# Decayed attention and a highway feed-forward on one core: a common ring of five PSUM banks, a written-out task order, and loads in pieces

## The chip, the cores and the metric

The kernel runs on one core of a Trainium2 chip. The metric is the time of one execution on the device, in microseconds (us), of the slowest core, which is the only one here. TensorE is called PE, VectorE DVE, ScalarE ACT, GpSimd POOL, and SP issues the transfers.

The executions scatter. The kernel before took 116.45 to 116.64 us in the three runs given at the start, but 114.9 to 119.2 us in the 33 runs made beside the experiments. So times are compared between kernels that ran on the same chip in the same session; where that wasn't possible, the text says so.

## The reference, cut to what matters

Four sequences of 768 positions with eight heads of 64 go through attention with a decay per head, in blocks of 64 with a running state. The output, as 3072 tokens of 512 features, goes through a highway layer.

```python
for b in range(nb):                                   # blocks of 64 positions
    intra = einsum('bhic,bhjc->bhij', qb, kb) * Dmask # scores, decayed, causal
    intra = einsum('bhij,bhjd->bhid', intra, vb)
    inter = einsum('bhid,bhde->bhie', qb * lam_pow, kv_state)
    out[:, :, sl] = intra + inter
    kv_state = lam_block * kv_state + einsum('bhsd,bhse->bhde', kb * rev_pow, vb)
...
H = maximum(x @ w_h, 0);  T = sigmoid(x @ w_t + b_t)  # x: 3072 x 512
return T * H + (1 - T) * x
```

## The kernel before

The tokens are taken in 12 chunks of 256, three to a sequence. Each chunk `n` passes through these tasks, on the engines named:

- load of k, q, v (SP), their cast or scaling to bf16 (`kb`, `qb`, `vs`: mostly POOL), transposition of k and q (PE) and copies `kT`, `qT` out of PSUM (ACT);
- scores (PE), masked by DVE into `m`; the products `inter` and `intra` into the tile `o` (PE), the state `kv` (PE) and its copy `ss` (ACT);
- copy of `o` to `xT` (ACT and DVE), then four feed-forward blocks `h`, `t` (PE), the sigmoid of `t` (ACT), `hmx` = max(h,0) − x (DVE), the product `th` = sigmoid × hmx (DVE for the first half, POOL for the second), the output turn x + th (PE), its copy `o_sb` (ACT), and the store (SP).

PSUM is divided into eight tiles of 512 fp32 values per partition, called banks below: scores own two, a ring of three (`"w"`) serves transpositions, blocks and turns, `o` has two and `kv` one.

```python
WB = 3
...
buf(("s", n, u), "s", [128, 2, 2, J, C], F32, pool=ps)          # scores: two banks of their own
buf((x + "tr", n, p), "w", [128, z // 2, J, C], bufs=WB, pool=ps)
buf((x, g, js[0]), "w", [128, 2, z * C], F32, bufs=WB, pool=ps) # h and t of a block
buf(("x", n, m, i), "w", [C, DM // parts_o], F32, bufs=WB, pool=ps)
```

The second is that a sigmoid whose product runs on DVE is written back into its PSUM bank, so this bank of the ring comes free only after block, sigmoid and product:

```python
def gate(g, js):
    return ("t_sb" if TH[js[0] // 2] == "POOL" else "t"), g, js[0]   # "t" is the PSUM tile
```

A list scheduler, run while the program is built, starts on each engine the task with the best key; the keys are in `K`.

```python
k = (max(0.0, s - free[e] - GAP), (t.key if t.key > -9 else 99)
     + SAME * (t.mode != last_mode) + WAIT * (s - free[e]))          # for PE
...
for t in plan(tasks):
    t.emit()
```

The loads: one transfer of 512 KB for each of k, q, v of a chunk (of 256 KB in the first two chunks), and 24 fills of four 128-column matmuls that warm PE up.

## Time and profile before

| | kernel before |
|---|---|
| time, median of 3 | 116.52 us |
| span of the profiled execution | 113.2 us |
| PE busy | 101.2 us (89%) |
| DVE, ACT, POOL busy | 67.7, 76.5, 69.6 us |
| instructions | 4880 |
| moved by DMA | 27.57 MB, mean 243 GB/s |

One of the page's costliest groups shows how a group is read: line, engine, operation, output<-inputs, shapes, count; then busy time and mean ns of one; then the engine's idle time before the group and what ended most of it.

```profile
L375 DVE TENSOR_TENSOR m<-s,tri 128x512 bf16<-128x512 f32 x48 | 31.6, 686 | 14.7 <-PE s L371 14.7
```

DVE stood idle 14.7 us in front of its masks, until the scores came from PE. This is room, not a limit. The limit is PE, and the prediction shows the views that say so.

Lines are told as L422 and the like. The ones that return are the block (L422 before, L293 after), the output turn (L444, L315), the transposition (L355, L223), scores (L371, L239), the mask (L375, L243), the product `th` (L438, L309), the state (L404, L272), the inter product (L384, L252), copies and casts on DVE and POOL (L306, L175), copies on ACT (L304, L173), loads (L341, L208) and stores (L456, L324).

### The profile page before, as it was taken

To read this page: it belongs to the slowest core of one execution; us is meant where nothing else is said; L and a number is where in the kernel's file an instruction comes from. 1 tells how busy PE (TensorE), PEld (TensorE's weight loads), DVE (VectorE), ACT (ScalarE), POOL (GpSimd) and SP (SyncE) were. 2 spreads that over 40 slices of the span, in tenths; PEclk is the share of its full clock that TensorE was granted. 3 is DMA by queue.
4 is the path that set the end of the run, shared out by engine and by line. 5 is a ranking of instruction groups with operands and counts; after the bars stand their busy time and mean duration, and the time that the engine had idled before them with its cause. 6 is when DMAs were issued, how large, how long until landed. Compare 5 with 4: busy or idle time off the path is not lost.

```text
span 113.2 us, 4880 instructions
## 1 busy us (share of the span) xinstructions
PE 101.2 (89%) x2145; PEld 88.9 (78%) x2145; DVE 67.7 (60%) x113; ACT 76.5 (68%) x146; POOL 69.6 (61%) x61
## 2 busy tenths in 40 slices
PE   4896576998897999999999999999999999998860
PEld 4895364778686788989889898998998989888750
DVE  0237756475266759658495676774966749764420
ACT  3595681556877676694879686967878667377550
POOL 6032337238999987979997997969597300404220
PEclk9999996799999999999999999999999999999999
DMA  0999999999999999999999999999951040403154
GB/s 9 255 298 291 311 329 349 302 263 300 279 296 291 336 352 306 293 288 298 307 320 310 285 340 294 333 285 298 337 184 53 11 180 6 184 7 148 37 208 162
DMA packets 43484, 27.57 MB, mean 243 GB/s; under 512 B 1348, under 2 KB 40520, under 8 KB 43464
## 3 DMA queue, kind: packets, MB, share of 16 engines
q1 hardware_dynamic: 43312, 27.27, 84.4%
q8 instruction: 16, 0.26, 1.0%
q14 instruction: 4, 0.03, 0.1%
q10 hardware_dynamic: 152, 0.01, 0.1%
HBM read 20.98 MB, written 6.29 MB: 241 GB/s over the span
## 4 chain that ended last, share of the span: by engine, by line
PE 72%; SPq 8%; DVE 7%; DMA 5%; ACT 3%; issue 2%; POOLq 1%; ACTq 0%
PE w L422 37%; PE w L444 9%; PE w L355 8%; SPq L341 7%; PE o L396 6%; DMA vf<-in_v_dram 5%; PE s L371 5%; PE o L384 5%; PE kv L404 4%; DVE m L375 3%; ACT w L435 2%; DVE xT L306 2%; DVE th L438 1%; SPq L300 1%; POOLq L602 1%
## 5 line engine op out<-in xcount | busy, mean ns | idle before, releaser
L422 PE MATMUL w<-xT,w_b 128*128 128x256 bf16 (+1 forms) x416 | 47.8, 267 | 1.4 <-DVE th L438 0.9
L422 PEld LDWEIGHTS <-w_b 128*128 128x128 bf16 x416 | 37.1, 99 | 6.5 <-issue 1.9
L375 DVE TENSOR_TENSOR m<-s,tri 128x512 bf16<-128x512 f32 x48 | 31.6, 686 | 14.7 <-PE s L371 14.7
L438 POOL TENSOR_TENSOR th<-t_sb,hmx 128x512 bf16<-128x512 bf16 (+1 forms) x13 | 14.0, 1080 | 21.2 <-DVE hmx L426 14.8
L349 POOL TENSOR_TENSOR qb<-qf,pow_q 128x1024 bf16<-128x1024 f32 (+1 forms) x13 | 22.1, 1703 | 7.8 <-DMA qf<-in_q_dram 7.7
L426 DVE SCALAR_TENSOR_TENSOR hmx<-w,xT 128x512 bf16<-128x512 f32 (+1 forms) x26 | 16.8, 647 | 10.0 <-PE w L422 5.2
L349 POOL TENSOR_TENSOR vs<-vf,pow_k 128x1024 bf16<-128x1024 f32 (+1 forms) x11 | 20.1, 1824 | 2.3 <-DMA vf<-in_v_dram 2.3
L450 ACT ACTIVATE o_sb<-w 128x512 f32<-128x512 f32 (+1 forms) x24 | 13.6, 587 | 5.3 <-PE w L444 5.0
L435 ACT ACTIVATE w<-w,bt_col 128x256 f32<-128x256 f32 (+1 forms) x26 | 11.2, 432 | 8.3 <-ACT kT L304 4.0
L304 ACT ACTIVATE qT<-w 128x1024 bf16<-128x1024 bf16 (+1 forms) x14 | 12.7, 904 | 4.8 <-PE w L355 4.8
L306 POOL CAST kb<-kf 128x1024 bf16<-128x1024 f32 (+1 forms) x11 | 11.0, 997 | 6.3 <-DMA kf<-in_k_dram 6.3
L304 ACT ACTIVATE kT<-w 128x1024 bf16<-128x1024 bf16 (+1 forms) x14 | 12.6, 896 | 1.9 <-PE w L355 1.9
L444 PE MATMUL w<-id,th 128*128 128x128 bf16 x96 | 12.9, 219 | 0.6 <-POOL th L438 0.6
L444 PE MATMUL w<-id,xT 128*128 128x128 bf16 x96 | 13.0, 220 | 0.4 <-DVE th L438 0.4
L438 DVE TENSOR_TENSOR th<-w,hmx 128x512 bf16<-128x512 f32 (+1 forms) x13 | 8.4, 645 | 6.3 <-ACT w L435 6.3
L435 ACT ACTIVATE t_sb<-w,bt_col 128x256 bf16<-128x256 f32 (+1 forms) x26 | 10.5, 461 | 2.4 <-PE w L422 2.4
L371 PE MATMUL s<-qT,kT 64*64 64x128 bf16 x384 | 11.4, 219 | 0.3 <-DVE m L375 0.3
L404 PE MATMUL kv<-vs,kb 64*64 64x64 bf16 x320 | 9.5, 197 | 1.3 <-POOL vs L349 0.9
L444 PEld LDWEIGHTS <-th 128*128 128x128 bf16 x96 | 9.3, 98 | 1.4 <-POOL th L438 0.8
L413 ACT ACTIVATE ss<-kv 128x256 bf16<-128x256 f32 x20 | 7.7, 384 | 3.5 <-PE kv L404 3.5
L404 PEld LDWEIGHTS <-kb 64*64 64x64 bf16 x320 | 8.0, 111 | 2.4 <-issue 1.6
L444 PEld LDWEIGHTS <-xT 128*128 128x128 bf16 x96 | 9.2, 98 | 0.5
(43 smaller groups left out, 109.2 us busy)
## 6 DMA issues: line engine op xcount, KB each, us to landing
out_dram<-o_sb SPq DMA_DIRECT2D x23, 256.0 KB, 4.9
kf<-in_k_dram SPq DMA_DIRECT2D x10, 512.0 KB, 7.5
qf<-in_q_dram SPq DMA_DIRECT2D x10, 512.0 KB, 7.8
vf<-in_v_dram SPq DMA_DIRECT2D x10, 512.0 KB, 7.0
kf<-in_k_dram SPq DMA_DIRECT2D x4, 256.0 KB, 5.2
qf<-in_q_dram SPq DMA_DIRECT2D x4, 256.0 KB, 5.7
vf<-in_v_dram SPq DMA_DIRECT2D x4, 256.0 KB, 6.1
w_f<-in_moe_w_h_dram SPq DMA_DIRECT2D x4, 256.0 KB, 6.2
```

Of the source, the lines that this page charges most:

```text
L304: A.activation(dst, src, AF.Copy)
L306: ENG[eng].tensor_copy(dst, src)
L349: ENG[eng].tensor_tensor(dst[:, hs], in0=get(x, n, p).rearrange("p h (j d) -> p h j d", j=J), in1=pw[:, :, :, None].to_broadcast([128, hs. ...
L371: T.matmul(get("s", n, u)[half(b), e, i, j, :], lhsT=get("kT", n)[half(e), hp, j, half(b)], rhs=get("qT", n)[half(e), hp, b * C:(b + 1) * ...
L375: V.tensor_tensor(get("m", n, u)[:, e], in0=get("s", n, u)[:, e], in1=tri[:, None].to_broadcast([128, 2, J, C]), op=ALU.mult)
L404: T.matmul(get("kv", n // NST)[half(e), hp, :], lhsT=get("kb", n)[half(b), j, 2 * hp + e, :], rhs=get("vs", n)[half(b), 2 * hp + e, j, :], ...
L422: T.matmul(get(x, g, js[0])[:, i, :], lhsT=w[:, kc, j * 128:(j + 1) * 128], rhs=get("xT", g)[:, kc, :], start=(kc == 0), stop=(kc == KC - 1))
L426: V.scalar_tensor_tensor(get("hmx", g, js[0]), in0=get("h", g, js[0]), scalar=0.0, in1=get("xT", g)[:, js[0]:js[-1] + 1, :], op0=ALU.max, ...
L435: A.activation(get(*gate(g, js))[:, i, :], get("t", g, js[0])[:, i, :], AF.Sigmoid, bias=bt_col[:, j:j + 1])
L438: ENG[TH[js[0] // 2]].tensor_tensor(get("th", g)[:, js[0]:js[-1] + 1, :], in0=get(*gate(g, js)), in1=get("hmx", g, js[0]), op=ALU.mult)
L444: T.matmul(get("x", n, b, p)[:, (j - js[0]) * 128:(j - js[0] + 1) * 128], lhsT=get(x, g)[:, j, r * C:(r + 1) * C], rhs=id128, start=(j == ...
L450: A.activation(get("o_sb", n, b, p), get("x", n, b, p), AF.Copy)
```

## The change

The intent is to let the scores take their banks from a common ring, so that every bank works for every stage; to replace the scheduler by an order found by a search, with each copy placed on an engine that has time for it then; and to let data arrive in smaller pieces. The list `ORDER` (537 task numbers) and the scheduler (some 150 lines) are cut here.

```diff
-WB = 3
-NF = 24
+WB = 5
+NF = 12
...
-KE = "POOL"
-OE = ["ACT", "ACT"]
-XE = ["ACT", "DVE"]
-K = dict( q=2.90, k=1.05, ... )
+EN = dict(                  # engine of each task of a kind: A = ACT, V = DVE, G = POOL
+    cw="GVGGGAAA", ck2="VVGA", cq2="VVGG", cv2="VGVV", et2="VAAVAVAV", ss="AAVAAAAVAVAAAAVVAVAV", xT="VAVAAAAAAAAAAAAAAAAAAAAA",
+    eo="AVVAAAVAAVAVAVAAAAVAVA", ck="VAAGGAGVGG", cq="GVGGGGGGGG", cv="GGGGGGGGGG", et="AVAVAVVAVAAAAAAAAAAA", eo1="A", eo3="AA")
+ORDER = [34, 32, 20, 33, 21, 43, 22, 42, 23, 16, 44, 24, 25, 26, 83, ... 518, 533, 534, 519, 535, 536]
...
-        for i in range(4):
-            T.matmul(get("fill")[:, 0, i, :], lhsT=id128, rhs=id128, start=True, stop=True)
+        for i in range(2):
+            T.matmul(get("fill")[:, i], lhsT=id128, rhs=id128[:, None, :].to_broadcast([128, NP, 128]), start=True, stop=True)
...
-        nc.sync.dma_start(out=get(x, n, p), in_=src[b, hs, ...])
+        for h in range(hs.start, hs.stop, 4):
+            nc.sync.dma_start(out=get(x, n, p)[:, h - hs.start:h - hs.start + 4, :], in_=src[b, h:h + 4, ...])
...
-                        T.matmul(get("s", n, u)[half(b), e, i, j, :], lhsT=get("kT", n)[half(e), hp, j, half(b)],
+                        T.matmul(get("s", n, u, e)[half(b), i, j, :], lhsT=turned("k", n)[half(e), hp, b * C + j:(b + 1) * C:J],
...
-            buf(("s", n, u), "s", [128, 2, 2, J, C], F32, pool=ps)
+            for e in range(2):
+                buf(("s", n, u, e), "w", [128, 2, J, C], F32, bufs=WB, pool=ps)
...
-    for t in plan(tasks):
-        t.emit()
+    for i in ORDER:
+        t = tasks[i]
+        t.emit(t.eng)
```

In the new order chunk 2 is loaded ahead of all weights, and all stores are issued behind the last load. kT is now interleaved as qT was, so that one copy function serves both.

## The prediction

> **What bounds the kernel now.** I read the page's slices first, then the engines' busy time in stretches, then the chain that ended last, then the engine timelines of the first 45 and last 11 us. Rows: busy tenths of TensorE (PE), its granted clock, and the DMA share, 2.83 us a digit.
>
> ```profile
> PE   4896576998897999999999999999999999998860
> PEclk9999996799999999999999999999999999999999
> DMA  0999999999999999999999999999951040403154
> ```
>
> PE is patchy for some 45 us, half clocked in slices 7 and 8, then full, and falls off in the last three slices. DMA is full from 3 to 83 us. In stretches (PE, PEld, DVE, ACT, POOL busy):
>
> ```profile
> 24.40:36.00 11.60, 10.07 (x208) 8.67 (x210) 6.00 (x10) 8.48 (x15) 10.84 (x8) 1.00 1.08 284
> 36.00:45.00 9.00, 8.78 (x201) 7.37 (x191) 6.84 (x11) 6.48 (x13) 8.04 (x6) 1.00 1.15 331
> 45.00:102.50 57.50, 57.50 (x1290) 51.46 (x1290) 39.60 (x63) 42.74 (x82) 39.40 (x27) 1.00 0.79 229
> 102.50:110.00 7.50, 6.01 (x99) 5.41 (x95) 2.46 (x7) 5.18 (x14) 2.49 (x3) 1.00 0.37 138
> ```
>
> From 45 to 102.5 us PE is busy 57.50 of 57.50 us: it is the bound, and DVE (39.6) and ACT (42.7) have room. A better order can only win before 45 us, after 102.5 us, or by fewer changes between kinds of PE work. The chain of waits prices those:
>
> ```profile
> 18.58 1.87 PE w L422 x8
> ...
> 74.41 0.45 PE o L384 x12
> 74.97 0.22 PE s L371 x12
> 75.20 0.55 PE w L444 x8
> 75.75 0.45 PE w L355 x8
> 76.19 1.75 PE w L422 x16
> 77.94 0.57 PE o L396 x32
> 78.51 0.22 PE s L371 x16
> 78.74 0.24 PE kv L404 x16
> ```
>
> A block of the feed-forward (8 matmuls of 256 columns) costs 1.75/2 = 0.875 us, a transposition or output turn of 8 0.45, scores 0.22, the intra product 0.57, a state 0.24. The x8 turn that follows scores costs 0.55, so going from 64x64 to 128x128 work costs 0.10 us; the hole before 74.97 is of that size. At 18.58 a block took 1.87, twice 0.875: the cold clock.
>
> **PE's work** is the same before and after: 44 blocks x 0.875 = 38.5; 8 half blocks of the last chunk x 0.45 = 3.6; 24 turns x 0.45 = 10.8; transpositions 20 x 0.45 + 8 x 0.225 = 10.8; 24 scores x 0.22 = 5.3; 12 intra x 0.57 = 6.8; 20 states x 0.24 = 4.8; inter 8 x 0.45 + 4 x 0.225 = 4.5. Sum 85.1 us, against a span of 113.2. Counting groups in PE's timeline, 8.1 us of it is done at 24.3 us. Going back from the end (4.7 us left at 102.5; 54.4 in the 57.5 saturated us, after 31 changes at 0.10) leaves 26.0 done at 45.
>
> **What the Trainium skill says.** "TensorEngine Tiling (Array Packing)", Key Properties: "Mode switching requires drain". The trace agrees, 0.10 us each. "TensorE: Matmul & The Clock Gate", Part 1, the HAM clock gate: the clock halves after an idle window of about 3.4 us and returns after a busy one. The trace agrees: 0.81 and 0.85 mean clock in 15 to 25 us, the first block at 1.87. "PSUM — Partial Sum Buffer", PSUM bank collisions: access is to be guarded by semaphore per bank and quadrant, so a bank is handed on only when its reader is done; no run yet shows what a fifth bank of the ring is worth. "VectorE: DVE Perf Modes", Why PSUM operands drop a tier: fp32 from PSUM runs at 1x. The trace agrees: a 128x512 mask from PSUM takes 686 ns, so copies moved to DVE are not cheaper than on ACT (a 128x512 xT copy 683 against 593).
>
> **The change, part by part.** I numbered the tasks as the code creates them and read the new list per engine.
>
> *PSUM.* Before, scores own two banks and the rest rotates over three. Now score halves take two of five common banks. Steady PE had no holes before, so this is worth nothing there directly; it allows other orders, and can also stall: a bank comes free only when the task five places earlier has been read.
>
> *PE order.* Changes between kinds: 45 before after 24 us, counted in the timeline; 43 in the new list from the first block on. Gain 0.2 us at most.
>
> *Head.* Queries, keys and values of chunk 2 are now loaded ahead of all weights. Before, 256 KB landed each 0.886 us (first k cast at 5.36, the 22nd piece at 23.96). At this pace the first weight pair, pieces 19 and 20, lands at 22.2, with the cast 22.9; before, the first block ran at 18.58. Ahead of it stand 6.9 us of attention work. Following the new lists with measured durations: fills to 8.2, scores of chunk 0 at 10.2 and 11.0, four masks (0.66 apart) to 13.3, intra 0 at 13.4, states and inter of chunk 0 to 15.4; the last v of chunk 1 is scaled on DVE about 17.5, state 1 17.6, k2 transposed 21.2, intra 1 22.7, scores and state of chunk 2 to 24.2. First block about 24.4, with 6.9 us done where the kernel before has 8.1. Then no hole shows in the lists (the last weight cast, 28.1, is before its block at 28.9), while before had holes of 0.45, 0.45, 0.25, 0.39 and 0.2 in 24 to 38. The new order reaches 26.0 us of work at 24.4 + 19.1 + 11 changes x 0.10 = 44.6: 0.4 ahead. If its first two blocks start cold it loses up to 1.6; PE is sparse from 13 to 20, but busy from 20 on, so I take half, 0.8.
>
> *Middle.* 54.4 of work and 31 changes: 57.5 again. I allow 0.5 for new stalls.
>
> *Tail.* Before, PE needed 102.5 to 108.3 for about 3.8 us of work, waiting for sigmoids, products and xT (holes of 0.42 to 0.6). The new list puts turns of chunks 9 and 10 and both half chunks between the waits; I give it 4.1: gain 1.7. The last block to the end of the span stays 4.9 us (108.3 to 113.2): maximum, product on POOL, turn, copy, 128 KB store.
>
> *Fills.* 96 matmuls of 128 columns become 24 of 512: the same columns and 72 fewer instructions, off the path, but nothing now fills the holes between 8 and 13 us.
>
> *Loads.* 30 loads of 512 KB become 60 of 256 KB. The queue's issues already took 1.6 to 1.7 us each, the time of the data itself, at about 300 GB/s, so bandwidth stays the limit. All stores now stand behind the last load: loads end about 5.36 + 80 x 0.886 = 76 instead of 83, and twelve output buffers just hold the stores back. This feeds PE earlier, but PE is not starved after 45.
>
> *Engines.* xT leaves DVE (10 x 0.68), while 8 output copies, 7 state copies and some transposition copies come to it, together about +15: DVE about 83 us in all, ACT 79, POOL about 65. None passes PE's 85 plus 5 of changes, but DVE is near.
>
> Sum: 0.4 - 0.8 - 0.5 + 1.7 = 0.8 gained by my working; with everything on time 0.4 + 1.7 + 0.2 = 2.3, and up to 3.5 if the first block starts as soon as its weights are cast (22.9). A searched order has presumably placed the head better than my coarse walk, so I choose 1.9: 116.52 - 1.9 = 114.6.
>
> **Rivals.** First: the head wins more. For it, DMA alone would allow a first block 1.5 us sooner, and holes of 1.74 us stood between 24 and 38. Then 113. Second: the five-bank ring or DVE becomes the new wait. For it, DVE goes from 67.7 to some 83 us and scores now claim two ring places just when blocks hold theirs; against it, ACT and DVE had 15 us of room in the saturated stretch. A 0.3 us hole per chunk would give 3.6 back: 117 to 118. Third: held-back stores stall the copies. The 13th output copy needs the store of the first output, tenth in the store queue, done about 5.36 + 90 x 0.886 = 85, while its turn is ready near 83. ACT would then stand up to 2 us; PE has three tasks before it needs that bank, so up to 1 us: 115.5. Fourth: the transfers are hidden anyway and PE's 85.1 + 4.5 fills the middle as before; then only the tail moves, 115.
>
> **Range and chances.** The saturated middle caps the gain: about 3.5 us in head and tail. 2% is 2.33 us, a little beyond my centre. Range 112.6 to 116.6. Faster by over 2%: 0.42. Within 2%: 0.52. Slower by over 2%: 0.06, needing stalls in the middle that the old order did not have.
>
> **What would show it.** Right: first block near 24 us, PE without holes from about 29 us, its timeline from there to the last blocks the sum of work and 0.10 us changes, the last block done 1 to 3 us before 108.3, no store before about 72 us, and 4.9 us from last block to end. Wrong: PE waiting in the middle for DVE masks, for a copy that holds a bank, or ACT for a store; a cold clock past 27 us; or a first block before 22 us, which would mean that loads in smaller pieces land faster than 0.886 us per 256 KB.

## The result, and the profile after

The kernel after took a median of 112.6 us (four runs, 112.3 to 113.4) against 116.5 us of the kernel before (four runs, 115.3 to 116.6). The ratio is 0.970, with a 95% interval of 0.962 to 0.978: faster by over 2%. A ratio is the mean time of one kernel's fast runs over that of the other's of the same rounds, so it is not quite the ratio of the medians. Two more sessions, below, gave 0.980 and 0.984, with intervals on both sides of 0.98: that the kernel is faster is shown three times, that it is so by over 2% only in this first measurement.

The profiled executions differ by less than these medians: spans of 113.2 and 110.9 us, 2.3 us apart. What follows divides these 2.3 us among the stages.

| | before | after |
|---|---|---|
| PE busy | 101.2 us (89%) | 101.5 us (92%) |
| DVE, ACT, POOL busy | 67.7, 76.5, 69.6 us | 78.4, 72.9, 63.5 us |
| instructions | 4880 | 4776 |

The slices of the kernel after (40 of 2.77 us; busy tenths of PE, PE's granted clock, DMA share) answer to those in the prediction:

```profile
PE   4996489689999999999999999999999999999960
PEclk9999965559999999999999999999999999999998
DMA  0999999999999999999999999999995250024263
```

PE is full from slice 10 to 38, where before it was full from slice 14 to 36. But the clock is at half speed in slices 7 to 9, a longer and deeper dip than before. DMA stays full to slice 30, one slice longer, but now with stores at the end: the last load landed at 76.7 us, where before it was 84.5.

PE's work, 85.1 us in all by the prediction's sum, is the same in both kernels, so two traces can be laid over each other by asking when so much of it was done. I counted the matmuls in the traces with the same prices (0.109 us per 256-column matmul, 0.056 per matmul of a turn or a transposition, 0.014, 0.018, 0.015 and 0.028 per matmul of scores, intra, state and inter; fills at nothing).

| trace | first block starts | 8 us done | 26 us done | 77 us done | last block ends | end of span |
|---|---|---|---|---|---|---|
| before | 18.6 | 24.2 | 46.4 | 99.6 | 108.3 | 113.2 |
| after | 24.8 | 26.0 | 44.9 | 98.6 | 106.0 | 110.9 |
| after minus before (before rounding) | | +1.8 | −1.4 | −1.0 | −2.3 | −2.4 |

So the **head** (to 26 us of work) gained 1.4 us, the **middle** lost 0.4, the **tail** (77 us of work to the last block) gained 1.2, and what follows the last block gained 0.1. These three stretches are shown by the view that gives each engine's busy time in a window. Its columns are the window in us from the start of the span, its length, busy time and instructions of PE, PEld, DVE, ACT and POOL, the granted clock, the DMA share and GB/s. Of the kernel before:

```profile
18.60:46.40 27.80, 26.05 (x548) 21.78 (x548) 16.41 (x27) 19.12 (x35) 21.73 (x18) 0.95 1.12 305
46.40:99.60 53.20, 53.20 (x1203) 47.56 (x1204) 37.33 (x59) 39.04 (x75) 38.16 (x26) 1.00 0.82 239
99.60:108.30 8.70, 7.85 (x136) 7.34 (x125) 4.01 (x8) 6.43 (x17) 1.82 (x2) 1.00 0.17 62
```

And of the kernel after:

```profile
24.80:45.00 20.20, 20.20 (x387) 17.80 (x385) 17.13 (x26) 14.54 (x29) 15.38 (x13) 1.00 1.11 291
45.00:98.60 53.60, 53.60 (x1242) 47.37 (x1241) 40.53 (x64) 39.70 (x73) 36.05 (x24) 1.00 0.87 248
98.60:106.10 7.50, 7.50 (x133) 7.22 (x123) 4.56 (x10) 5.50 (x15) 1.82 (x2) 1.00 0.29 107
```

The new kernel starts its blocks 6.2 us later, and from then on PE is busy every moment until the last block (20.20 of 20.20, 53.60 of 53.60, 7.50 of 7.50). The old one idled 1.75 us in its head stretch and 0.85 in its tail.

How bad the new head still is shows in the same view of the kernel after, before the first block:

```profile
10.00:15.00 5.00, 2.72 (x101) 2.24 (x102) 4.47 (x9) 2.10 (x4) 3.48 (x4) 0.95 1.22 290
15.00:20.00 5.00, 4.68 (x109) 3.87 (x102) 3.25 (x7) 1.85 (x4) 1.90 (x1) 0.50 1.15 294
20.00:25.00 5.00, 4.04 (x82) 3.65 (x83) 4.09 (x6) 2.64 (x5) 2.40 (x2) 0.53 1.02 326
```

PE was busy only 2.72 of 5.00 us between 10 and 15 us, waiting mostly for casts and copies of k and q, and then ran at a clock of 0.50 although it was busy 4.68 of the next 5.00. The chain that ended last (start, us, what) has the price of it:

```profile
20.64 1.90 PE w L223 x16
22.54 0.02 issue
22.56 1.24 DVE qT L175
```

The two transpositions of chunk 2 took 1.90 us at L223, where 16 matmuls of a warm one cost 0.90 by the prediction's price, and they stand directly in the way of the first block.

### The profile page after: what moved, and what is told of

Read it like the earlier page. It is cut to its first block, busy times and chain, and to the rows that moved or that the text cites. A ratio compares the mean times of both kernels' runs of the same rounds, so it can differ in the third digit from the quotient of the medians.

```text
span 110.9 us, 4776 instructions
## 1 busy us (share of the span) xinstructions
PE 101.5 (92%) x2073; PEld 86.3 (78%) x2073; DVE 78.4 (71%) x128; ACT 72.9 (66%) x137; POOL 63.5 (57%) x55
## 4 chain that ended last, share of the span: by engine, by line
PE 76%; SPq 11%; DMA 6%; DVE 2%; issue 1%; POOLq 1%; ACT 0%; DVEq 0%
PE w L293 39%; SPq L208 11%; PE w L315 10%; PE w L223 10%; DMA kf<-in_k_dram 6%; PE w L239 5%; PE o L264 5%; PE kv L272 4%; PE o L252 4%; DVE qT L175 1%; POOLq L469 1%; DVE kb L175 1%; DVE hmx L297 0%; ACT o_sb L173 0%; DVEq L175 0%
## 5 line engine op out<-in xcount | busy, mean ns | idle before, releaser
L293 PE MATMUL w<-xT,w_b 128*128 128x256 bf16 (+1 forms) x416 | 46.9, 265 | 0.0
L293 PEld LDWEIGHTS <-w_b 128*128 128x128 bf16 x416 | 36.5, 98 | 4.4
L243 DVE TENSOR_TENSOR m<-w,tri 128x512 bf16<-128x512 f32 x48 | 30.8, 684 | 4.2 <-PE w L239 3.8
L309 POOL TENSOR_TENSOR th<-t_sb,hmx 128x512 bf16<-128x512 bf16 (+1 forms) x13 | 15.1, 1165 | 23.5 <-DVE hmx L297 14.4
L217 POOL TENSOR_TENSOR qb<-qf,pow_q 128x1024 bf16<-128x1024 f32 (+1 forms) x11 | 19.2, 1746 | 4.2 <-DMA qf<-in_q_dram 4.2
L173 ACT ACTIVATE xT<-o 128x512 bf16<-128x512 f32 x22 | 12.1, 597 | 3.7 <-PE o L264 2.3
L173 ACT ACTIVATE kT<-w 128x1024 bf16<-128x1024 bf16 (+1 forms) x11 | 10.0, 906 | 6.9 <-PE w L223 6.9
L239 PE MATMUL w<-qT,kT 64*64 64x128 bf16 x384 | 12.8, 231 | 0.7 <-ACT kT L173 0.3
L173 ACT ACTIVATE o_sb<-w 128x512 f32<-128x512 f32 (+1 forms) x17 | 9.6, 575 | 4.8 <-PE w L315 4.6
L223 PE MATMUL w<-id,kb 128*128 128x128 bf16 x96 | 8.5, 231 | 2.8 <-DVE kb L175 1.4
L272 PE MATMUL kv<-vs,kb 64*64 64x64 bf16 x320 | 10.4, 203 | 0.1
L239 PEld LDWEIGHTS <-kT 64*64 64x64 bf16 x384 | 9.1, 112 | 1.2 <-ACT kT L173 0.5
(46 smaller groups left out, 118.9 us busy)
```

What stands on the lines that cost most here:

```text
L173: A.activation(dst, src, AF.Copy)
L217: ENG[eng].tensor_tensor(dst[:, hs], in0=get(x, n, p).rearrange("p h (j d) -> p h j d", j=J), in1=pw[:, :, :, None].to_broadcast([128, hs. ...
L223: T.transpose(get(x + "tr", n, p)[:, i, j, :], get(x + "b", n)[:, j, h:h + 2, :], id128)
L239: T.matmul(get("s", n, u, e)[half(b), i, j, :], lhsT=turned("k", n)[half(e), hp, b * C + j:(b + 1) * C:J], rhs=turned("q", n)[half(e), hp, ...
L243: V.tensor_tensor(get("m", n, u)[:, e], in0=get("s", n, u, e), in1=tri[:, None].to_broadcast([128, 2, J, C]), op=ALU.mult)
L272: T.matmul(get("kv", n // NST)[half(e), hp, :], lhsT=get("kb", n)[half(b), j, 2 * hp + e, :], rhs=get("vs", n)[half(b), 2 * hp + e, j, :], ...
```

## The experiments

Twelve kernels ran in three sessions, each on another chip, each beside eleven runs of the kernel before; all were correct. All but the first and the ninth are edits of the kernel after.

| run | session | median us | ratio to before (95%) |
|---|---|---|---|
| after_again | 1 | 113.42 | 0.980 (0.975 to 0.986) |
| after_old_tail | 1 | 113.97 | 0.984 (0.977 to 0.991) |
| old_order | 1 | 115.61 | 0.997 (0.988 to 1.006) |
| old_new_tail | 1 | 115.16 | 0.998 (0.991 to 1.005) |
| after_own_banks | 2 | 123.47 | 1.046 (1.038 to 1.054) |
| old_order_ring5 | 2 | 114.21 | 0.984 (0.979 to 0.989) |
| after_one_load | 2 | 114.16 | 0.983 (0.979 to 0.988) |
| after_warm | 2 | 112.84 | 0.969 (0.963 to 0.975) |
| after_third | 3 | 113.51 | 0.984 (0.968 to 0.999) |
| after_tuned | 3 | 112.66 | 0.975 (0.968 to 0.983) |
| after_stores_early | 3 | 114.50 | 0.990 (0.980 to 1.000) |
| after_old_engines | 3 | 115.98 | 1.003 (0.991 to 1.015) |

Against the kernel before and a margin of 2%, after_warm counts as faster and after_own_banks as slower; the other ten are unclear by that measure, though an interval that ends below 1 still means faster.

### The kernel after once more

The spans were 2.3 us apart and the medians 3.9, so the first question was how much is scatter. No edit.

> The changed kernel as it is, to see how far both kernels scatter. The two traces differ by 2.3 us of span (113.2 against 110.9) but the medians by 3.9 (116.48 against 112.6). Theory A: the trace of before fell on one of its quick executions (115.27); over more rounds its times spread by over 1 us while those of after stay within 1, and the mean gain is 3.0 to 3.8. Theory B: the trace shows the usual gain; then 2.3 to 2.7.

The median was 113.42 us against 116.73, the means of the fast runs 113.32 against 115.65, a gain of 2.3 us. That is the gain of the traces, and not the 3.9 us of the first measurement's medians. The kernel before is the noisy one: over the three sessions its spans went from 112.8 to 117.2 us, and those of the kernel after, the first measurement included, only from 110.5 to 113.3. A low clock explains a part of this (ten executions of before with a mean clock under 0.96 averaged 115.6 us of span, the 23 others 114.3), but one of 117.0 us had a clock of 0.97. Why it scatters stays open. For the kernel after the clock goes further: its three executions with a mean clock of 0.94 took 114.6 to 115.1 us, the 13 others, with 0.945 to 0.954, 112.3 to 113.7. By my estimate a mean that is lower by 0.015 over 112 us is one more spell of 3.4 us at half clock.

### The new order with the old end, and the old order with the new end

My prediction gave the tail's gain to the new order at the end. Two kernels exchange the part of the list after the last intra product, with its engines.

```diff
 # after_old_tail: only the part of ORDER after the last intra product, and the engines of four copies in it
-xT="...AAAA", eo="...AAAAVAVA", eo3="AA"
+xT="...AAAV", eo="...AAAAAAAA", eo3="AV"
```

> The changed kernel, but what follows the last intra product is issued in the old order, with its old engines. Theory: the tail holds 2.0 of the 2.3 us by which the spans differ, so this is 1.7 to 2.3 us slower than after, about 114.5. Rival: the old tail's holes came from a late start of its inputs; then under 0.7 us slower.

It took 113.70 us on average, 0.4 more than the kernel after on the same chip. In its trace the tail lasted 7.4 us, as in the kernel after. So the order at the end is worth next to nothing, and the theory that gave it the tail fell. The old order, for the next two runs, is the list that the scheduler of the kernel before makes, written out and run by the code of the kernel after, with the old engines and the old division of PSUM.

```diff
 # old_order
-WB = 5
+WB = 3
-ORDER = [34, 32, 20, ...]      EN = dict(cw="GVGGGAAA", ...)
+ORDER = [32, 42, 33, ...]      EN = dict(cw="VGAVAGGV", ..., et="AAAA...", ss="AAAA...", ck="GGGG...")
-                buf(("s", n, u, e), "w", [128, 2, J, C], F32, bufs=WB, pool=ps)
+                buf(("s", n, u, e), "s", [128, 2, J, C], F32, bufs=2, pool=ps)
```

> The code of after (loads in two pieces, 24 wide fills, kT rows interleaved, one-bank score halves) with the whole order, the engines and the split of PSUM banks of before (scores two, the rest three). Theory: order is everything, so as before within 0.5 us, about 116.3. Rival: the pieces of the loads or the fills carry part of the gain, then 115.5 or less.

This kernel has the loads in pieces, the wide fills and the interleaved kT of the kernel after, and it ran like the kernel before (0.997). These three parts together show no gain with the old order; the interval would let 1.2% hide. old_new_tail is old_order with the new end of the list.

> The run before this one, but with the new order and engines after the last intra product. Theory: the tail alone gives 1.7 to 2.3 us over old_order, and nothing before it moves. Rival (the tail gain needs the new order ahead of it, which leaves other work over): under 1 us.

It averaged 115.27 us against 115.20 of old_order, and its tail lasted 8.8 us, as in before and old_order (8.7). The tail's gain came with neither end of the list. Of the things exchanged so far, only the banks were left.

### The two divisions of PSUM

Each order was now run with the other division. First the new order with banks as before:

```diff
 # after_own_banks
-WB = 5
+WB = 3
-                buf(("s", n, u, e), "w", [128, 2, J, C], F32, bufs=WB, pool=ps)
+                buf(("s", n, u, e), "s", [128, 2, J, C], F32, bufs=2, pool=ps)
```

> The changed kernel with the PSUM banks split as before: two for scores alone, three for the rest. In the traces so far PE takes 7.4 us from 77 of its 85.1 us of work to the last block with five common banks (old tail order or new), and 8.7 to 8.8 with three (old tail order or new). Theory R: in the tail no scores run, so their two banks lie idle and blocks wait for three; this run then takes 8.5 to 8.8 us there, and is slower than after by 1.2 us or more, also in the middle, where the new order counts on five. Rival O (the order made the tail): 7.4 again.

It was the slowest of all, 4.6% slower than the kernel before, with a mean of 121.3 us over its fast runs. Its profile fell into a slow execution (span 121.7 us; those of its fast runs were 118.9 to 119.6), so it is read for its waits alone. The largest waits of PE after 24 us (engine, line, what it waited for: us in total, times, longest):

```profile
PE s L239 <- DVE m L243: 2.0, 4, 0.8
PE w L293 <- DVE th L309: 0.8, 2, 0.4
PE w L293 <- DVE qT L175: 0.6, 2, 0.4
PE w L315 <- DVE th L309: 0.5, 1, 0.5
```

Scores wait for masks to leave the two banks, and blocks (L293) wait for a product on DVE to leave one of three. With four smaller ones these waits come to some 5 us. The kernel's fast runs are about 8 us above those of the kernel after on other chips (113.3 and 113.6), so a part of the loss is not accounted for; the trace also has the first block late, at 27.5 us. The new order spreads scores among the blocks in a way that needs whichever bank comes free. Then the old order with the common ring, old_order_ring5, which is old_order with these two lines put back:

> The code of after with the whole order and engines of before, but five common banks. Theory R: the tail falls from 8.7 to about 7.5 us, nothing else moves by over 0.5: 1.2 us quicker than old_order (about 114.5). Rival O: the tail stays at 8.7.

It came to 0.984 of the kernel before, where old_order had come to 0.997 in the session before it. The two ran on different chips and their intervals just touch, so the size of this step is uncertain. But 0.984 is also what the kernel after reached in its two repeats (0.980 and 0.984), and on this chip old_order_ring5 averaged 114.26 us, the kernel after with whole loads (after_one_load, next) 114.06: by the times, the ring under the old order brings most of the gain, and what the new order and engines add to it is not resolved. The tail of the two traces, however, can be compared directly, since both run the same list there. PE's timeline of old_order (start, us, engine, line, operation, count; in brackets the idle time before and what ended it):

```profile
103.68 1.95 PE L293 MATMUL w<-xT,w_b 128*128 128x128 bf16 x32
106.05 1.50 PE L293 MATMUL w<-xT,w_b 128*128 128x128 bf16 x24 [0.42 <-DVE th L309]
...
108.42 0.22 PE L315 MATMUL w<-id,xT 128*128 128x128 bf16 x1 [0.43 <-DVE th L309]
...
108.87 0.61 PE L293 MATMUL w<-xT,w_b 128*128 128x128 bf16 x8
```

And of old_order_ring5:

```profile
103.39 3.29 PE L293 MATMUL w<-xT,w_b 128*128 128x128 bf16 x56
...
107.41 0.61 PE L293 MATMUL w<-xT,w_b 128*128 128x128 bf16 x8
```

With three banks PE does 32 of 56 matmuls of the last half chunks and stops until DVE has made a product. The next matmuls are a block, which doesn't read a product: what it waited for is the bank, held by a `t` until the product has read it. In the middle of the next turn PE stops again, for the value of a product that comes late now. With five banks all 56 run in one piece. Counted from their start, the last block begins 4.02 us later (107.41 − 103.39) in place of 5.19 (108.87 − 103.68). Scores are over by then, so in the old division two banks stand empty while PE waits for one of the three others. The same split runs through all traces: the tail took 8.7 to 8.8 us in three with three banks in the ring (before, old_order, old_new_tail; after_own_banks, in its slow execution, had 8.2), and 7.4 us in all ten with five, under either order.

In the middle, from 30 to 77 us of work, old_order_ring5 was 1.1 us slower than old_order (50.3 against 49.2). POOL delivered a `qb` late twice there, and PE waited 0.45 and 0.74 us for it. So part of what the ring gave was lost again in this profiled run.

### The loads

> The changed kernel with each of the 30 big loads as one DMA of 512 KB again. Theory: bandwidth sets the landing, so the time stays within 0.5 us of after. Rival (halves land sooner or keep the queue fuller): over 1 us slower, with k of chunk 2 landing after 20.5 us instead of 19.8.

```diff
 # after_one_load
-        for h in range(hs.start, hs.stop, 4):
-            nc.sync.dma_start(out=get(x, n, p)[:, h - hs.start:h - hs.start + 4, :], in_=src[b, h:h + 4, ...])
+        nc.sync.dma_start(out=get(x, n, p), in_=src[b, hs, ...])
```

It averaged 114.06 us, with no run of the kernel after on that chip to set it against; on two other chips that had averaged 113.32 and 113.60. The ratios, 0.983 against 0.980 and 0.984, say the same. The pieces are worth 0.7 us at the most and perhaps nothing: not resolved. The trace has two holes of PE of 0.22 and 0.73 us near 51 and 56 us for which the profile shows no releaser, and the kernel after has none there, but one trace does not make them the pieces' work.

### The cold clock

If the clock of 0.50 in front of the first block costs what it seems to, work that keeps PE busy should win it back. Five groups of fills, 22 matmuls of 512 columns in all, each group in a turn of the ring of its own, were put where PE had waited.

```diff
 # after_warm
+WARM = [6, 2, 2, 4, 8]
...
+    def warm(i, n):
+        for _ in range(n):
+            T.matmul(get("warm", i), lhsT=id128, rhs=id128[:, None, :].to_broadcast([128, NP, 128]), start=True, stop=True)
+    for i, n in enumerate(WARM):
+        buf(("warm", i), "w", [128, NP, 128], F32, bufs=WB, pool=ps)
+        task("fill", lambda eng, i=i, n=n: warm(i, n), writes=[("warm", i)])
```

> The changed kernel with 22 more idle matmuls of 512 columns, put into PE's holes between 11 and 20 us, so that the clock should not fall (it is half from 14 to 23 us in the trace of after). Theory: the transpositions of chunk 2 (1.9 us for both) take 0.9, the first block comes 1.0 to 1.4 us sooner (about 23.5), and the end moves by that much: 112.2. Rival: the first block waits for data, not for the clock, and the fills only delay: no gain.

The window view of its trace:

```profile
15.00:20.00 5.00, 5.00 (x121) 3.22 (x114) 3.32 (x7) 1.85 (x4) 1.90 (x1) 1.00 1.19 296
```

and its chain, where L421 are the added fills and L203 the same transpositions as above:

```profile
19.22 1.83 PE w L421 x8
21.05 0.91 PE w L203 x16
...
21.98 1.24 DVE qT L155
```

The clock stayed at 1.00, the transpositions took 0.91 us in place of 1.90, the first block started at 23.85, 0.95 us earlier than in the kernel after, and the span ended at 109.8 against 110.9. With 0.969 (mean 112.35 us) it is the best ratio. So about 1 us still lay in the head of the kernel after. The fills take PE's time themselves: the transpositions start at 21.05, the moment at which the last eight fills end, so they may have waited for them. A second trace agrees on the clock without fills: in after_stores_early (below), whose list is that of the kernel after up to there, the half clock happened to end at 21.4 us in place of 24.7, and the first block started at 23.8 in place of 24.8.

### The kernel after once more, and a version tuned from it

The third session began with a baseline of its own.

> The changed kernel once more, so that the next three have it on their own chip. As before: 0.97 to 0.98 of the kernel before, 112.5 to 113.7, the tail from 77 us of work to the last block 7.4 us.

It took 113.51 us, ratio 0.984, with spans of 111.1 to 112.7; only two of the eleven runs of the kernel before counted as fast, so its interval is wide. after_tuned keeps the fills but shortens the last group from eight to three, transposes q of chunk 2 before k, gives three tasks of the head to other engines, and puts the very last product on DVE.

```diff
 # after_tuned (beside five groups of fills as in after_warm)
+WARM = [6, 2, 2, 4, 3]
-    cw="GVGGGAAA", ... cv="GGGGGGGGGG", et="AVAVAVVAVAAAAAAAAAAA"
+    cw="GVGGGAAG", ... cv="VGGGGGGGGG", et="AAAVAVVAVAAAAAAAAAAA"
+    def on_of(g, js):                      # the last half chunk's products both on DVE
+        return "DVE" if g == N else TH[js[0] // len(js) % 2]
```

> The changed kernel with idle matmuls that hold the clock up to 20 us, with q of chunk 2 transposed ahead of k (it lands 2 us earlier), its copy on ACT, v of chunk 2 scaled on DVE, one weight cast on POOL, and the last product on DVE. Theory: first block at 23.2 (after 24.8, with the fills alone 23.85), last block to end 4.5 (4.9), so 2 us less than after: 110.5 to 111.5. Rival: what PE gains at the first blocks is lost to the weights' landing (last cast about 28), then 112 to 112.5.

It averaged 112.64 us, 0.8% under after_third on the same chip, and its ratio was 0.975, so it is faster than both kernels. But it didn't do what was hoped over after_warm. The first block started at 24.51, not the 23.2 expected, and the profile's list of PE's waits after 24 us has why:

```profile
PE w L218 <- ACT kT L152: 1.0, 1, 1.0
```

With q turned first, the copy of k on ACT became the last thing the scores wait for. The last product on DVE brought 4.8 us from the last block to the end of the span in place of 4.9: nothing to speak of.

### The stores early again

after_stores_early puts each store back among the loads, where its output is ready.

```diff
 # after_stores_early: the store tasks in ORDER moved up among the loads; nothing else
```

> The changed kernel with nine of its stores put back between the loads, as the kernel before has them, instead of all behind the last load. Theory: PE is not short of data after 45 us, so within 0.5 us of after, with the loads ending some 7 us later (about 82). Rival: holding the stores back is what feeds the middle, then over 1 us slower, with PE waiting for POOL's scaled q, k or v.

It averaged 114.34 us, 0.7 more than after_third; the two intervals overlap. SP's timeline shows the price (a group of issues: start, us, line, what):

```profile
68.41 1.66 SPq L208 DMA_DIRECT2D kf<-in_k_dram  x2
70.17 2.41 SPq L324 DMA_DIRECT2D out_dram<-o_sb  x2
72.68 1.18 SPq L208 DMA_DIRECT2D qf<-in_q_dram  x2
```

The two stores held the queue for 2.41 us, in part waiting for a copy that was not done, and the loads behind them waited too. PE then stood 2.2 us, once, for a cast of k on POOL:

```profile
PE w L223 <- POOL kb L175: 2.2, 1, 2.2
```

The stores of the kernel after, in one group behind all loads, cannot do this:

```profile
72.61 35.88 SPq L324 DMA_DIRECT2D out_dram<-o_sb  x25
```

So holding the stores back seems worth something to this order, as far as this placement of them goes; other executions than the profiled one were not looked into. How much of it is the transfer of the data and how much the blocked queue was not separated.

### The new order on the old engines

> The new order and banks, but every task on the engine that it had before (all transposition and output copies and states on ACT, xT alternating, all casts of k on POOL). Theory: the new order's places in the ring are timed for the spread engines, so this stalls PE by 0.2 to 0.5 us a chunk, 2 to 5 us in all. Rival: engines have room enough (DVE 39.6 and ACT 42.7 of 57.5 us in the middle before) and it stays within 1 us of after.

```diff
 # after_old_engines: EN alone
-    cw="GVGGGAAA", ck2="VVGA", ... et2="VAAVAVAV", ss="AAVAAAAVAV...", ... ck="VAAGGAGVGG", ... et="AVAVAVVAVA..."
+    cw="VGAVAGGV", ck2="VGVA", ... et2="AAAAAAAA", ss="AAAAAAAAAA...", ... ck="GGGGGGGGGG", ... et="AAAAAAAAAA..."
```

It averaged 115.82 us, 2.2 more than after_third, and was no faster than the kernel before (1.003). The theory that each chunk would lose a little fell: from 30 to 77 us of work it took 49.4 us, as after_third did. The whole loss of the trace lies in the head, where 26 us of work were done at 47.5 in place of 45.5 and 30 us at 52.4 in place of 49.9. PE's waits after 14 us begin with two for state copies on ACT:

```profile
PE kv L272 <- ACT ss L173: 1.0, 1, 1.0
PE o L252 <- ACT ss L173: 0.8, 1, 0.8
```

It is tempting to read the loss from these two. But both lie before 20 us, and the first block was not late: 25.23 us against 25.40 in after_third. What was slow are the first two blocks themselves. PE's timeline of after_old_engines, and below it of after_third:

```profile
25.23 3.60 PE L293 MATMUL w<-xT,w_b 128*128 128x256 bf16 x16
25.40 1.92 PE L293 MATMUL w<-xT,w_b 128*128 128x256 bf16 x16
```

The granted clock was 0.50 until 28.7 us, against 23.9 in after_third, and this makes 1.7 of the 2.0 us lost up to 26 us of work. Whether the waits kept the clock down was not tested. Nor is it the whole story: two other executions of this kernel took 116.3 and 116.5 us at a mean clock of 0.948 and 0.947, where the kernel after, on another chip, took 113.5 and 113.7 at 0.948. So the old engines cost time under this order, and why stays open. In the middle of this trace the engines of the copies made no difference.

## Why the prediction was right or wrong

**The size was near, the sum was not.** The prediction, 114.6 us, is a ratio of 0.984. The first measurement's 112.6 lay at the lower edge of the range, the two repeats gave 0.980 and 0.984. But the centre held a guess of 1.1 us "presumably", and two of the terms beside it were wrong in opposite ways: the working itself gave 0.8 us. That the chosen centre came so near is partly luck.

**What held.** The first block came at 24.8 us (24.4 was worked out). From 24.8 to 98.6 us PE had no hole. The middle lost 0.4 us (0.5 allowed). The loads ended at 76.7 us (76 said). The last block ended 2.3 us before 108.3, and 4.9 us of the span were left after it. No store was issued before 72.6 us. The third rival, copies stalled by held-back stores, did not come: PE never waited for one. The engines came out at 78, 73 and 64 us for DVE, ACT and POOL (83, 79 and 65 said), with none at PE's level. Of the rivals, the first, that the head wins more, came nearest, but by the holes between 24 and 38 us that went; the first block came no sooner.

**"Steady PE had no holes before, so this is worth nothing there directly."** This step failed by what it left out. In the middle no trace shows a gain from the ring, but the sentence ended the search. In the tail, when scores are over, the old division leaves two banks unused, and three banks make PE wait 0.42 and 0.43 us for banks and products; the ring alone takes 1.2 us out (tail of 8.7 to 8.8 us in three traces, 7.4 in ten). And the new order cannot live without it: with three banks and two it took 121.3 us on average, some 8 us more.

**"The new list puts turns of chunks 9 and 10 and both half chunks between the waits; I give it 4.1: gain 1.7."** The gain of the tail was there, 1.2 us and not 1.7, but its cause was not: the old end under the new ring had a tail of 7.4 us, the new end under the old division one of 8.8. The holes in the timeline were read as waits for sigmoids and products. They were, but behind them stood a bank: a wait for a product says who released PE, not whether PE wanted the product or its place.

**The head: "0.4 − 0.8".** It gained 1.4 us instead of losing 0.4. The term of 0.4 rested on the old kernel having 26.0 us of work done at 45 us. Counted from the trace it had 24.8: the back-reckoning from the end took 0.10 us for each of 31 changes and 4.7 us left at 102.5, where 0.087 and 5.5 are measured. That error is worth 1.2 us. The new kernel's 26 us of work came at 44.9, between the 44.6 worked out and the 45.4 with cold blocks, so nearly the whole error lies in where the old kernel stood. The term of 0.8, cold first blocks, did not come in the profiled execution: the two first blocks took 1.85 us together, warm (in after_old_engines they did run cold, 3.60 us). The cold clock lay over the attention work ahead of them instead, and after_warm shows that it cost about 1.0 us. Its effect is contained in the first block's time; that this was nevertheless near 24.4 is luck, since the walk through the lists left the cold clock out. The prediction also let the trace agree with a clock that halves after an idle window of 3.4 us. The half clock is in the trace, the idle window isn't: no hole of PE before the clock fell at 18.1 us was over 1.2 us.

**What makes the head better** the prediction left to a guess. The traces must be compared at a like clock. Where the clock stayed at 1.00 from 8 us on, 26 us of work were done at 46.0 and 46.2 under the old order (old_new_tail, old_order_ring5), and at 44.0 and 44.8 under the new one (after_warm and after_tuned, with their fills). With spells of half clock it was 46.4 and 47.5 under the old order (before and old_order, spells of 3.4 and 6.8 us in all), and 44.8 to 45.6 under the new one (after, after_again and after_third, 10.2 us). So the new order with its engines is ahead, and the ring under the old order isn't. On the old engines the new order was at 47.5, but with 1.7 us of that from cold blocks; the old order on the new engines did not run. How order and engines share the gain stays open.

**The changes between kinds of work** cost 0.09 us each on average in both kernels (31 and 41 of them in the saturated stretches), so that term was right to 0.01, and the new order saves none. One of the two readings behind it was wrong: the "hole before 74.97" is no hole, but four short groups of inter and scores matmuls that the shortened view of the chain leaves out.

**What stays open**: why the kernel before scatters by over 4 us; whether pieces of 256 KB matter; and the shares of ring, order and engines in the time, as the ring with the old order (0.984) can't be told from the repeats of the whole change (0.980 and 0.984).

## What to carry to other kernels

When PE waits for a buffer, ask whether other buffers are idle at that time: a split of PSUM that is right for the steady state can be wrong at the end, where a stage is over and its banks stand empty, and one common ring serves both. An order and its buffers are one design: the order searched for five common banks was 4.6% slower than the old kernel on the old split, and on the old engines it was no faster than the old kernel. And before giving a gain to a change of order, run the old order on the new buffers, since a wait's line in one trace does not say whether the engine wanted a value or its place.

## What the Trainium skill lacked or had wrong

- "PSUM — Partial Sum Buffer" gives the rules for sharing a bank, but neither it nor another page says how many banks a rotation needs. Here the same list of tasks had a tail of 8.7 us with three banks beside two idle ones and 7.4 us with five in common, because a block's bank is held through sigmoid and product.
- "TensorE: Matmul & The Clock Gate", Part 1, the HAM clock gate, has the clock halve after an idle window of about 3.4 us and return after a busy one. The page also reports, in "A second HAM failure mode: psum-queue depth-cycling", a kernel whose clock went up and down because PE paused briefly and often. What is lacking is how much of a window may be idle. Here no hole of PE between 8 and 20 us was over 1.4 us, yet the clock fell to 0.50 after a stretch with PE busy 2.72 of 5.00 us, and it stayed there while PE was busy 4.68 of the next 5.00. With fills (busy 5.00 of 5.00) it stayed at 1.00. How much filling is just enough was not found.
- "TensorEngine Tiling (Array Packing)", Key Properties, names the drain at a change of mode but no cost: 0.10 us at a change in the chain, 0.09 us on average over 31 and 41 changes.
- "DMA: Bandwidth & Descriptors", Bandwidth, has the rule to batch transfers to 1 MiB or more. Between 40 and 60 us the kernel after, with pieces of 256 KB, and after_one_load, with transfers of 512 KB, both moved 291 GB/s: with many transfers under way no loss is to be seen at a quarter of that size against a half. No run here had 1 MiB.
